# One stage of a fused attention and expert kernel: four of seven products summed in one accumulation bank, groups of products interleaved, result memory opened at another point

## The chip, the cores and the metric

One core of one Trainium2 chip runs the whole kernel as one program. The metric is the time of one execution on the device in microseconds (us). Five engines matter, each with its own queue of instructions that it takes in order: TensorE (PE in the rows; PEld are its weight loads), VectorE (DVE), ScalarE (ACT), GpSimd (POOL) and SyncE (SP, which here only issues transfers). They meet through semaphores.

## The reference, cut to what matters

Attention with normed queries and keys, then a routed expert layer (each token goes to one of 8 experts), then a bilinear layer. The change lies in the bilinear layer alone:

```python
def _moe2_ref(x, w1, w2, w3, w_out):      # x: 1792 x 768
    a = x @ w1                            # 768 x 1024
    b = x @ w2                            # 768 x 1024
    h = a * b @ w3                        # 1024 x 1024
    return (h @ w_out).astype(np.float32) # 1024 x 768
```

## The kernel before, in words

Numbers are carried as pairs of 16-bit floats (high part, low part), so a product of two matrices is three matmuls: high by high, low by high, high by low. `mm3` (line 940) issues these for three blocks of 128 rows, nine matmuls to an accumulation bank ("a product" below). There are eight banks (`mm_p`, tile name psm), handed out in turn; each holds 512 numbers per partition.

`w3 @ w_out` is formed early in the program. The last stage (line 1433, tiles pso) multiplies it by the elementwise product `a * b`, which lies in tiles `ab0` to `ab7`, also as pairs. The stage in front of it, the one that is changed, computes `a` and `b` and their elementwise product. It does so block by block with seven products in the place of eight, after a scheme of sums and differences of the four quarters of each operand. The operand from x is split into quarters by rows of x and by tokens. The seven forms of it are the tiles `b_0` to `b_6` (T1, T2, T3, T4, B11, B21, B22 in the code), and there is a set for each of two groups of tokens: s=0 with 2 x 384 tokens and s=1 with 2 x 512. The set for s=0 is ready before the stage starts, that for s=1 is made in the stage by `operands(1)`: a difference on VectorE (lines 1055, 1065, 1066, 1067, on tile `y`), a high part on ScalarE (line 1050), a low part on VectorE (line 1053). The seven forms of a weight block are the tiles `m2w`, three tiles (j = 0, 1, 2) for each pair (fp, z): fp = 0 to 3 counts blocks of columns, z = 0 stands for w1 and z = 1 for w2. A piece (fp, z, j) is made in four steps: three VectorE instructions rebuild 32-bit numbers from the loaded 64-bit ones (lines 205 to 207, tile `y32w`), four small sums follow (lines 1165 to 1168, on GpSimd, or on VectorE for four early pieces), ScalarE writes the high part (line 1175), and VectorE the low part (line 1182). The pieces of fp = 0 are ready when the stage starts; the other 18 are made in it.

Work that feeds later products is a generator, `steps()`, whose items carry a place ("gate") from which they may be issued and a cost. After each product the code calls `fill(slot, us)`, which lets the generator go on while its gate is reached and a credit of time is left; `force(key)` issues what is missing of a weight block at the point where the first product needs it. What results is the order of each engine's queue, and it is fixed: every instruction stays behind the one written before it on its engine.

Before, `half(fp, s)` does 14 products, one group of seven for z = 0 and one for z = 1, group after group in the order A11, S2, S3, S1, A12, A22, S4. The first four take a bank each. A12, A22 and S4 are then added in the banks of A11, S3 and S1. ScalarE copies the first product out (line 1368, tiles ua and ub), and VectorE forms all sums with it: five additions per group (lines 1329 and 1331) that read a bank. VectorE also multiplies a by b (lines 1349 and 1386), four instructions per half. `done` writes the pair into `ab`: high part on ScalarE (line 1345), low part on GpSimd (line 1346). The tiles `ab1` to `ab7` lie where `y` lay, so `open_ab` can be called only when `operands(1)` has been issued in full.

## Time and profile before

| what | us |
|---|---|
| median of 3 timed runs (967.3 to 971.01) | 970.12 |
| the profiled execution | 965.99 |
| its span in the trace | 964.1 |
| the changed stage in the trace (633.1 to 847.3) | 214.2 |
| the last stage, from there to the end of the span | 116.8 |

Of the span PE is busy 869.6 us (90%), DVE 647.2 (67%), ACT 476.9 (49%) and POOL 310.8 (32%). The rest of the program, before 633 us and after 847 us, is the same text in both kernels. A busy share is an average: in the stage that is changed the question is which engine PE waits for, and when.

### The profile page before, as it was taken

Reading aid. Unit: us, or ns where it says so; the run is one execution under the profiler, and the core shown is the slowest. Engines: PE = TensorE matmul, PEld = TensorE weight load, DVE = VectorE, ACT = ScalarE, POOL = GpSimd, SP = SyncE. Lnnn points to the kernel's source line nnn. Section 1 sums busy time; section 2 is a strip of 40 time slices with the busy share of each in tenths; the row PEclk is TensorE's granted clock in tenths of the full one; section 3 lists DMA queues with packets and bytes.
Section 4 is the critical chain, followed back from the end, with each engine's and each line's share of the span. In section 5 each row is a group of like instructions: output and inputs, shape, how many; then the busy total and the mean of one; then the engine's idle time right before and its main releaser. Section 6 shows DMA issues by size and latency. Waiting matters only on the chain.

```text
span 964.1 us, 19484 instructions
## 1 busy us (share of the span) xinstructions
PE 869.6 (90%) x7766; PEld 588.0 (61%) x7766; DVE 647.2 (67%) x956; ACT 476.9 (49%) x738; POOL 310.8 (32%) x325
## 2 busy tenths in 40 slices
PE   0498899999998979998999999997889899999996
PEld 0155566666665745776889999963444445456664
DVE  6988988878897776255556788999976766220000
ACT  4698788878887543343456766543322222110000
POOL 6367556767743224310101110002333423121111
PEclk9899899999999998999999999998999999999999
DMA  7858689797399974595788999611222211111111
GB/s 184 188 143 203 150 175 199 138 185 160 84 203 217 238 223 135 173 215 170 257 254 244 302 288 289 214 45 38 72 66 66 67 44 50 50 66 50 50 50 50
DMA packets 200351, 144.44 MB, mean 150 GB/s; under 512 B 139376, under 2 KB 178832, under 8 KB 200256
## 3 DMA queue, kind: packets, MB, share of 16 engines
q1 hardware_dynamic: 197248, 131.39, 53.1%
q0 software_dynamic: 3008, 11.76, 3.7%
q8 instruction: 63, 1.03, 0.5%
q14 instruction: 32, 0.26, 0.1%
HBM read 103.52 MB, written 14.18 MB: 122 GB/s over the span
## 4 chain that ended last, share of the span: by engine, by line
PE 41%; DVE 8%; issue 3%; DMA 1%; ACT 0%; POOLq 0%; DVEq 0%; SPq 0%; ACTq 0%
PE psm L940 30%; PE pso L1433 11%; DVE m2w L1182 1%; DVE y32w L206 1%; DVE y32w L205 1%; DVE y32w L207 1%; DMA xte<-xr 1%; DVE ua L1349 0%; DVE ua L1331 0%; DVE u L1331 0%; DVE b L1053 0%; DVE ub L1329 0%; DVE y L1067 0%; DVE y L1055 0%; ACT b L1050 0%
## 5 line engine op out<-in xcount | busy, mean ns | idle before, releaser
L940 PE MATMUL psm<-b,m2w 128*128 128x384 f16 (+1 forms) x1008 | 197.1, 359 | 17.2 <-DVE u L1331 8.9
L940 PEld LDWEIGHTS <-m2w 128*128 128x128 f16 x1008 | 99.9, 99 | 114.1 <-issue 15.7
L940 PE MATMUL psm<-ht,w2t 128*128 128x320 f16 (+7 forms) x1152 | 124.2, 270 | 0.0
L940 PEld LDWEIGHTS <-w1t 128*128 128x128 f16 x1152 | 109.5, 99 | 22.2 <-issue 4.5
L940 PEld LDWEIGHTS <-w2t 128*128 128x128 f16 x1152 | 109.0, 98 | 13.9
L940 PE MATMUL psm<-xte,w1t 128*128 128x288 f16 (+6 forms) x1008 | 106.3, 268 | 6.7 <-PEq L1027 4.2
L1433 PE MATMUL pso<-ww,ab 128*128 128x384 f16 x672 | 109.4, 326 | 0.0
L404 DVE TENSOR_REDUCE nm<-psm 128x2 f32<-128x896 f32 x84 | 88.6, 1084 | 12.9 <-PE psm L402 12.5
L461 PE MATMUL po<-vf,e 128*128 128x65 f32 (+1 forms) x576 | 90.0, 275 | 4.6 <-ACT w L227 4.6
L1433 PEld LDWEIGHTS <-ab 128*128 128x128 f16 x672 | 65.7, 98 | 43.6
L461 PEld LDWEIGHTS po<-vf,e 128*128 128x128 f32 (+1 forms) x576 | 71.2, 180 | 20.4 <-issue 12.1
L402 PE MATMUL psm<-kt,qt 64*64 64x448 f16 x336 | 47.5, 380 | 35.3 <-DMA qt<-qf 28.1
L723 POOL DMA_INDIRECT xr<-xd,ix x19 | 22.3, 1173 | 173.7 <-DMA ix<-md 159.1
L431 PE MATMUL pss<-qt,kt 64*128 64x448 f16 (+1 forms) x576 | 68.3, 379 | 10.6 <-DVE e L446 9.0
L1437 DVE TENSOR_SCALAR ob<-pso,meta_s 128x384 f32<-128x384 f32 x14 | 8.7, 618 | 99.3 <-PE pso L1433 93.4
L1130 DVE SCALAR_TENSOR_TENSOR w1t<-st,w1t 128x1024 f16<-128x1024 f32 x42 | 50.9, 1223 | 35.3 <-ACT w1t L1124 34.0
L464 PE MATMUL po<-v,e 128*128 128x65 f16 (+1 forms) x480 | 63.9, 195 | 1.7 <-DVE lacc L525 1.7
L465 PE MATMUL po<-vl,e 128*128 128x64 f16 (+1 forms) x480 | 63.8, 194 | 0.0
L466 PE MATMUL po<-v,e 128*128 128x65 f16 (+1 forms) x480 | 63.0, 194 | 0.0
L1436 ACT ACTIVATE ob<-pso,meta_s 128x384 f32<-128x384 f32 x14 | 8.1, 580 | 99.0 <-PE pso L1433 99.0
L446 DVE TENSOR_TENSOR e<-pss,e 128x896 f16<-128x896 f32 x48 | 51.7, 1083 | 6.5 <-ACT e L444 6.2
L464 PEld LDWEIGHTS <-e 128*128 128x128 f16 (+1 forms) x480 | 53.1, 115 | 4.7 <-issue 2.9
(266 smaller groups left out, 1647.9 us busy)
## 6 DMA issues: line engine op xcount, KB each, us to landing
st<-in_moe_w_dram SPq DMA_DIRECT2D x42, 512.0 KB, 5.0
st<-in_moe_w_dram SPq DMA_DIRECT2D x44, 384.0 KB, 4.9
st<-in_moe_w_dram SPq DMA_DIRECT2D x48, 256.0 KB, 3.3
w<-in_moe_w_dram SPq DMA_DIRECT2D x16, 512.0 KB, 4.6
w<-in_moe_w_out_dram SPq DMA_DIRECT2D x16, 384.0 KB, 3.8
xd<-rx SPq DMA_DIRECT2D x12, 448.0 KB, 4.1
kf<-in_k_dram SPq DMA_DIRECT2D x24, 192.0 KB, 3.5
qf<-in_q_dram SPq DMA_DIRECT2D x24, 192.0 KB, 3.1
```

Of the source, the lines that this page charges most:

```text
L402: nc.tensor.matmul(ps[h, z, 0:S], lhsT=s["q"][0][h, c:c + 64], rhs=s["k"][0][h, S * j:S * j + S], start=True, stop=True)
L404: nc.vector.tensor_reduce(s["nm"][:, t], ps[:, :, 0:S], axis=AX.X, op=ALU.max, negate=True)
L431: nc.tensor.matmul(ps[o, h, 0:S], lhsT=l, rhs=rt[HD[h], S * j:S * j + S], start=a == 0, stop=a == 3)
L446: nc.vector.tensor_tensor(lo, p, hi, op=ALU.subtract)
L461: nc.tensor.matmul(ov[r, t, :], lhsT=e[0], rhs=vfs[i % 2][:, h, c, 0:D + 1], start=z == 0, stop=z == 3)
L464: nc.tensor.matmul(ov[r, t, :], lhsT=e[0], rhs=vh, start=z == 0, stop=False)
L465: nc.tensor.matmul(ov[r, t, 0:D], lhsT=e[0], rhs=s["vl"][:, h, c, :], start=False, stop=False)
L466: nc.tensor.matmul(ov[r, t, :], lhsT=e[1], rhs=vh, start=False, stop=z == 3)
L723: nc.gpsimd.indirect_dma_start(out=dst, out_offset=None, in_=xd, in_offset=bass.IndirectOffsetOnAxis(ap=ix[0:dst.shape[0], t:t + 1], axis=0))
L940: nc.tensor.matmul(ps, lhsT=x, rhs=y, start=first and j == 0, stop=last and j == n - 1, **kw)
L1130: nc.vector.scalar_tensor_tensor(t[:, 1], st, 32.0, t[:, 0], op0=ALU.mult, op1=ALU.subtract)
L1433: nc.tensor.matmul(pp[z], lhsT=ab[f][:, x, ts], rhs=ww[f][:, y, z * 384:(z + 1) * 384], start=f == 0 and x == 0 and y == 0, stop=f == 7 an ...
```

## The change

A group of seven products now uses three banks. A11, S2, S3 and A22 are added up in one, in this order, and ScalarE copies the running sum out behind each of the first three (and behind A22 for z = 0), line 1340, into tiles named c11, c12, c22 and c21 (all shown as `c` in the rows, with a number). S1 and then S4 are added up in the second, A12 has the third. VectorE makes three additions per group (lines 1344 and 1346): A12 onto c11, S1 onto c22, S1 + S4 onto c12. The multiplications stay four per half (lines 1354 and 1373). The seven products of a group have the places 0, 1, 3, 5, 6, 9 and 11, groups start 7 places apart, and all products are issued in the order of their places, so that two groups alternate on PE: A11, S1, A22 of the group before, S2, S4 of the group before, A12, S3. The gates of z = 1 weight pieces become 25 + 3j in the place of 24 + 4j, and the estimate in `fill` is another one. `open_ab` is called after step 11 of `operands(1)` instead of 12, and results for `ab1` to `ab7` that are ready before that wait in a list (`late`) and are written out one per product afterwards.

The new code, without the removed lines (they stand in the kernel above):

```diff
+            yield 28 * (fp - 1) + (25 + 3 * j if z else 8 + 6 * j if fp > 1 else 0), c
+    ab = [ab0p.tile([P, 2, NT], F16, name="ab0")]
+    pending, late = [], []
+    made_by = {A11: 2, S1: 5, S2: 7, A12: 9, S3: 8, A22: 11, S4: 3}
+    def done(f, cs, x):
+        if f >= len(ab):
+            late.append((f, cs, x))
+            return
+        nc.scalar.activation(ab[f][:, 0, cs], x, AF.Copy)
+        nc.gpsimd.tensor_tensor(ab[f][:, 1, cs], x, ab[f][:, 0, cs], op=ALU.subtract)
+    def group(fp, s, z, a):
+        stt, tt = nc.vector.scalar_tensor_tensor, nc.vector.tensor_tensor
+        c1, c2 = halves(s)
+        n = PC[s][1]
+        r = 1.0 if z else 1.0 / 256
+        bk, x = {}, {}
+        def read(k, name, ps):
+            x[k] = temp(name, s)
+            nc.scalar.activation(x[k], ps, AF.Copy, scale=r)
+        def add(k, ps):
+            if z:
+                tt(x[k], ps, x[k], op=ALU.add)
+            else:
+                stt(x[k], ps, r, x[k], op0=ALU.mult, op1=ALU.add)
+        def end(k, slot):
+            if not z:
+                a[k] = x[k]
+                return
+            def finish():
+                tt(x[k], a[k], x[k], op=ALU.mult)
+                done(fp + 4 * (k >= 2), (c1, c2)[k % 2], x[k])
+            pending.append((slot, finish))
+        def run(slot, p, ps):
+            if p == A11:
+                read(0, "c11", ps)
+            elif p == S2:
+                read(1, "c12", ps)
+            elif p == S3:
+                read(3, "c22", ps)
+                pending.append((slot + 1, lambda: (add(3, bk[1]), end(3, slot + 2))))
+            elif p == A12:
+                add(0, ps)
+                end(0, slot)
+            elif p == S4:
+                add(1, ps)
+                end(1, slot + 1)
+            elif p == A22 and z:
+                tt(a[2], ps, a[2], op=ALU.mult)
+                done(fp + 4, c1, a[2])
+            elif p == A22:
+                read(2, "c21", ps)
+                a[2] = x[2]
+        of = {A11: (0, B11, True), S1: (1, T1, True), S2: (0, T2, False), A12: (2, B21, True), S3: (0, T3, False),
+              A22: (0, T4, False), S4: (1, B22, False)}
+        last = fp == SB - 1 and s and z
+        at = {A11: 0, S1: 1, S2: 3, A12: 6 if last else 5, S3: 5 if last else 6, A22: 9, S4: 11}
+        def product(slot, p):
+            if p == A11:
+                force((fp, z))
+            w = wst2[fp, z]
+            while fp == 0 and s and len(done2) < made_by[p]:
+                one()
+            b, o, first = of[p]
+            if first:
+                bk[b] = bank(n)
+            cs = slice(p * P, (p + 1) * P)
+            mm3(bk[b], [(w[j][:, 0, cs], w[j][:, 1, cs], bt[s][o][:, 0, j], bt[s][o][:, 1, j]) for j in range(3)], first, True,
+                skip_group_check=not first)
+            run(slot, p, bk[b])
+            if len(done2) >= 11 and len(ab) == 1:
+                open_ab()
+            if late and len(ab) > 1:
+                done(*late.pop(0))
+            pending.sort(key=lambda q: q[0])
+            while pending and pending[0][0] <= slot:
+                pending.pop(0)[1]()
+                pending.sort(key=lambda q: q[0])
+            fill(slot, 9 * n * .000425 - (.1 + n * .0006))
+        return [(at[p], p, product) for p in at]
+    line = []
+    for g in range(4 * SB):
+        if g % 2 == 0:
+            a = {}
+        line += [(7 * g + t, p, f) for t, p, f in group(g // 4, g // 2 % 2, g % 2, a)]
+    for slot, p, f in sorted(line, key=lambda q: q[0]):
+        f(slot, p)
+    while pending:
+        pending.pop(0)[1]()
+        pending.sort(key=lambda q: q[0])
```

ScalarE's queue at the start of the stage. Before (ua, a and ub are copies out of a bank; b are high parts of the operands for s=1):

```order
L1368 ACTIVATE ua<-psm 128x384
L1050 ACTIVATE b_4_9769<-y_5815 128x1536
L1050 ACTIVATE b_6_9771<-y_5815 128x1536
L1390 ACTIVATE a_9848<-psm 128x384
L1050 ACTIVATE b_0_9765<-y_5815 128x1536
L1368 ACTIVATE ub<-psm 128x384
L1050 ACTIVATE b_1_9766<-y_5815 128x1536
L1345 ACTIVATE ab_9781<-a_9848 128x384
```

After the change, from the same place:

```order
L1340 ACTIVATE c_9792<-psm 128x384
L1050 ACTIVATE b_4_9769<-y_5815 128x1536
L1050 ACTIVATE b_6_9771<-y_5815 128x1536
L1340 ACTIVATE c_9823<-psm 128x384
L1050 ACTIVATE b_0_9765<-y_5815 128x1536
L1340 ACTIVATE c_9847<-psm 128x384
L1340 ACTIVATE c_9860<-psm 128x384
L1050 ACTIVATE b_1_9766<-y_5815 128x1536
L1340 ACTIVATE c_9884<-psm 128x384
```

The operand copies stay in their order (four of the seven are shown), but beside them stand five copies out of banks in the place of three: they follow A11, S2 and S3 of the first group, A11 of the second and A22 of the first.

VectorE's queue where the last operand form for s=1 (b_3, T4) and the first weight piece of fp=1 (y32w from st_9794) are made. Before:

```order
L1053 TENSOR_TENSOR b_3_9768<-y_5815,b_3_9768 128x1536
L205 TENSOR_SCALAR y32w<-st_9794 128x512
L206 SCALAR_TENSOR_TENSOR y32w<-st_9794,y32w 128x512
L207 SCALAR_TENSOR_TENSOR y32w<-st_9794,y32w 128x512
L1165 TENSOR_TENSOR y32w<-y32w 128x128
L1166 TENSOR_TENSOR y32w<-y32w 128x128
L1167 TENSOR_TENSOR y32w<-y32w 128x128
L1168 TENSOR_TENSOR y32w<-y32w 128x128
L1349 TENSOR_TENSOR c_9823<-c_9823,c_9908 128x384
L1331 SCALAR_TENSOR_TENSOR u_10025<-psm,ua 128x512
```

After the change:

```order
L1053 TENSOR_TENSOR b_3_9768<-y_5815,b_3_9768 128x1536
L1344 TENSOR_TENSOR c_9896<-psm,c_9896 128x384
L205 TENSOR_SCALAR y32w<-st_9794 128x512
L206 SCALAR_TENSOR_TENSOR y32w<-st_9794,y32w 128x512
L207 SCALAR_TENSOR_TENSOR y32w<-st_9794,y32w 128x512
L1165 TENSOR_TENSOR y32w<-y32w 128x128
L1166 TENSOR_TENSOR y32w<-y32w 128x128
L1167 TENSOR_TENSOR y32w<-y32w 128x128
L1168 TENSOR_TENSOR y32w<-y32w 128x128
L1346 SCALAR_TENSOR_TENSOR c_9947<-psm,c_9947 128x512
L1354 TENSOR_TENSOR c_9896<-c_9823,c_9896 128x384
```

Before, the addition u_10025, which frees the bank into which the next product A22 is to be added, stands behind the piece and behind a multiplication. After, the two additions around the piece (c_9896, c_9947) read banks that no later product is added into.

VectorE's queue up to the low part (line 1182) of the last weight piece for fp=1, z=1, the second m2w row in the first fence, the only one in the other. Before:

```order
L1331 SCALAR_TENSOR_TENSOR ua<-psm,ua 128x384
L1331 SCALAR_TENSOR_TENSOR u_10263<-psm,ua 128x384
L1331 SCALAR_TENSOR_TENSOR u_10263<-psm,u_10263 128x384
L1182 SCALAR_TENSOR_TENSOR m2w<-y32w,m2w 128x896
L205 TENSOR_SCALAR y32w<-st_10182 128x512
L206 SCALAR_TENSOR_TENSOR y32w<-st_10182,y32w 128x512
L207 SCALAR_TENSOR_TENSOR y32w<-st_10182,y32w 128x512
L1331 SCALAR_TENSOR_TENSOR c_10262<-psm,ua 128x384
L1331 SCALAR_TENSOR_TENSOR ua<-psm,ua 128x384
L1182 SCALAR_TENSOR_TENSOR m2w<-y32w,m2w 128x896
L1329 TENSOR_TENSOR ub<-psm,ub 128x384
```

After the change:

```order
L1344 TENSOR_TENSOR c_10117<-psm,c_10117 128x512
L205 TENSOR_SCALAR y32w<-st_10175 128x512
L206 SCALAR_TENSOR_TENSOR y32w<-st_10175,y32w 128x512
L207 SCALAR_TENSOR_TENSOR y32w<-st_10175,y32w 128x512
L1346 SCALAR_TENSOR_TENSOR c_10192<-psm,c_10192 128x384
L1354 TENSOR_TENSOR c_10117<-c_9983,c_10117 128x512
L1182 SCALAR_TENSOR_TENSOR m2w<-y32w,m2w 128x896
L1346 SCALAR_TENSOR_TENSOR c_10292<-psm,c_10292 128x384
```

The three instructions of the rebuilding in front of that low part belong to fp=2 in both. Of the additions of the group fp=1, s=0, z=0 five stand in front of it before, and one after.

## Rows read from the trace of the kernel before

**Rows 1.** Stretches: us, busy PE, PEld, DVE, ACT, POOL (count), PE clock, DMA, GB/s

```profile
633.10:847.30 214.20, 196.96 (x1011) 99.90 (x1009) 155.93 (x216) 55.96 (x81) 65.07 (x86) 0.97 0.17 56
...
637.20:707.50 70.30, 59.04 (x299) 29.78 (x296) 65.58 (x88) 22.54 (x28) 17.09 (x20) 0.93 0.21 67
```

**Rows 2.** Timeline of PE in the stage: start, us, what, [idle before <- releaser]

```profile
633.16 8.94 PE L940 MATMUL psm<-b,m2w 128*128 128x384 f16 x54
642.28 21.71 PE L940 MATMUL psm<-b,m2w 128*128 128x384 f16 x117 [0.18 <-DVE u L1331]
669.84 26.71 PE L940 MATMUL psm<-b,m2w 128*128 128x512 f16 x126 [5.85 <-ACT ab L1345]
701.05 5.72 PE L940 MATMUL psm<-b,m2w 128*128 128x384 f16 x25 [4.50 <-DVE u L1331]
707.53 43.78 PE L940 MATMUL psm<-b,m2w 128*128 128x384 f16 x227 [0.76 <-DVE m2w L1182]
753.41 4.22 PE L940 MATMUL psm<-b,m2w 128*128 128x384 f16 x25 [2.09 <-DVE u L1331]
759.40 43.78 PE L940 MATMUL psm<-b,m2w 128*128 128x384 f16 x227 [1.77 <-DVE m2w L1182]
805.27 42.20 PE L940 MATMUL psm<-b,m2w 128*128 128x384 f16 x207 [2.09 <-DVE u L1331]
```

**Rows 3.** Stretches of PE: us, busy (count), PE clock, DMA share, GB/s

```profile
669.00:673.00 4.00, 3.16 (x8) 0.50 0.39 131
757.00:761.00 4.00, 2.23 (x14) 1.00 0.41 135
805.00:809.00 4.00, 3.73 (x16) 0.69 0.00 0
```

**Rows 4.** Timeline of DVE before the first long wait of PE ends

```profile
664.11 1.76 DVE L1053 TENSOR_TENSOR b<-y,b 128x1536 f16<-128x1536 f32 x1 [1.55 <-ACT b L1050]
665.79 0.42 DVE L205 TENSOR_SCALAR y32w<-st 128x512 uint32<-128x512 uint32 x1
...
668.63 0.55 DVE L1349 TENSOR_TENSOR c<-c,c 128x384 f32<-128x384 f32 x1
669.10 0.68 DVE L1331 SCALAR_TENSOR_TENSOR u<-psm,ua 128x512 f32<-128x512 f32 x1
```

**Rows 5.** Timeline of DVE: start of its run, and ends of two waits for fp=1

```profile
637.21 1.75 DVE L1055 TENSOR_TENSOR y<-y 128x1536 f32<-128x1536 f32 x1
...
685.48 1.08 DVE L1182 SCALAR_TENSOR_TENSOR m2w<-y32w,m2w 128x896 f16<-128x896 f32 x1
...
701.10 0.56 DVE L1331 SCALAR_TENSOR_TENSOR u<-psm,u 128x384 f32<-128x384 f32 x1
...
706.14 1.33 DVE L1182 SCALAR_TENSOR_TENSOR m2w<-y32w,m2w 128x896 f16<-128x896 f32 x1
```

**Rows 6.** Groups of DVE by form in 633 to 848: busy us, mean ns, idle before

```profile
L1329 DVE TENSOR_TENSOR ub<-psm,ub 128x512 f32<-128x512 f32 x8 | 5.5, 691 | 6.1 <-PE psm L940 6.0
...
L1331 DVE SCALAR_TENSOR_TENSOR ua<-psm,ua 128x384 f32<-128x384 f32 x8 | 4.4, 555 | 2.3 <-PE psm L940 2.1
```

**Rows 7.** Lines 1182 and 1329 alone: count, shortest/median/longest in ns

```profile
L1182 DVE SCALAR_TENSOR_TENSOR m2w<-y32w,m2w x21: 1080/1089/2053, 619.3 to 807.0; 128x896 f16<-128x896 f32 x21
...
L1329 DVE TENSOR_TENSOR ub<-psm,ub x16: 545/622/692, 646.9 to 847.5; 128x384 f32<-128x384 f32 x8, 128x512 f32<-128x512 f32 x8
```

**Rows 8.** Groups of ACT by form in 633 to 848

```profile
L1175 ACT ACTIVATE m2w<-y32w 128x896 f16<-128x896 f32 x18 | 17.0, 943 | 14.5 <-POOL y32w L1168 11.2 <-DVE y32w L1168 3.3
...
L1390 ACT ACTIVATE a<-psm 128x512 f32<-128x512 f32 x4 | 2.4, 594 | 18.6 <-PE psm L940 18.6
```

**Rows 9.** Timeline of ACT at the start of the stage

```profile
636.08 0.47 ACT L1368 ACTIVATE ua<-psm 128x384 f32<-128x384 f32 x1
636.45 2.85 ACT L1050 ACTIVATE b<-y 128x1536 f16<-128x1536 f32 x2
```

**Rows 10.** Waits in 620 to 850: who for whom, us in total, times, longest

```profile
ACT ab L1345 <- DVE a L1386: 46.8, 8, 7.9
```

More of the change, by code (lines that the diff above doesn't have):

```diff
@@ L1305, in steps @@
             fp, z, j = pieces[min(k, len(pieces) - 1)]
-            yield 28 * (fp - 1) + (24 + 4 * j if z else 8 + 6 * j if fp > 1 else 0), c
-    ab = []
-    ab = []
-    def half(fp, s):
-        stt, tt = nc.vector.scalar_tensor_tensor, nc.vector.tensor_tensor
-        c1, c2 = halves(s)
-        n = PC[s][1]
-        r = 1.0 / 256
-        slot = 14 * (2 * fp + s)
-        us, ev = 9 * n * .000425, .2 + n * .00099
-        def product(ps, w, a, o, first):
-            cs = slice(a * P, (a + 1) * P)
-            while slot == 15 and len(done2) < 7:
-                one()
-            mm3(ps, [(w[j][:, 0, cs], w[j][:, 1, cs], bt[s][o][:, 0, j], bt[s][o][:, 1, j]) for j in range(3)], first, True,
-                skip_group_check=not first)
-        def add(out, ps, x, z):
-            if z:
-                tt(out, ps, x, op=ALU.add)
-            else:
-                stt(out, ps, r, x, op0=ALU.mult, op1=ALU.add)
-        def rest():
-            nonlocal slot
-            while slot == 15 and len(done2) < 12:
-                one()
-            if len(done2) == 12 and len(ab) == 1:
-                open_ab()
-            while pending and pending[0][0] <= slot:
-                finish(*pending.pop(0)[1:])
-            fill(slot, us - ev)
-            slot += 1
-        def done(f, cs, x):
-            nc.scalar.activation(ab[f][:, 0, cs], x, AF.Copy)
-            nc.gpsimd.tensor_tensor(ab[f][:, 1, cs], x, ab[f][:, 0, cs], op=ALU.subtract)
-        def finish(f, cs, x, y):
-            tt(x, x, y, op=ALU.mult)
-            done(f, cs, x)
-        a = {}
-        def end(z, k, x):
-            if z:
-                when = slot + 1 if fp or s else {(0, 1): 14, (1, 0): 15, (1, 1): 17}[k]
-                pending.append((when, fp + 4 * k[0], (c1, c2)[k[1]], a[k], x))
-                pending.sort(key=lambda p: p[0])
-            else:
-                a[k] = x
-        for z in range(2):
-            force((fp, z))
-            w = wst2[fp, z]
-            p1 = bank(n)
-            product(p1, w, A11, B11, True)
-            u = temp("ub" if z else "ua", s)
-            nc.scalar.activation(u, p1, AF.Copy, scale=1.0 if z else r)
-            rest()
-            ps = bank(n)
-            product(ps, w, S2, T2, True)
-            add(u, ps, u, z)
-            rest()
-            p3 = bank(n)
-            product(p3, w, S3, T3, True)
-            x21, t1 = temp("c21", s), temp("u3", s)
-            add(t1, p3, u, z)
-            rest()
-            p4 = bank(n)
-            product(p4, w, S1, T1, True)
-            add(t1, p4, t1, z)
-            end(z, (1, 1), t1)
-            rest()
-            product(p1, w, A12, B21, False)
-            if z:
-                tt(a[0, 0], p1, a[0, 0], op=ALU.mult)
-                done(fp, c1, a[0, 0])
-            else:
-                a[0, 0] = temp("a11", s)
-                nc.scalar.activation(a[0, 0], p1, AF.Copy, scale=r)
-            rest()
-            product(p3, w, A22, T4, False)
-            add(x21, p3, u, z)
-            end(z, (1, 0), x21)
-            rest()
-            product(p4, w, S4, B22, False)
-            add(u, p4, u, z)
-            end(z, (0, 1), u)
-            rest()
@@ L1401, in fused_kernel @@
-    pending = []
-    ab.append(ab0p.tile([P, 2, NT], F16, name="ab0"))
+            yield 28 * (fp - 1) + (25 + 3 * j if z else 8 + 6 * j if fp > 1 else 0), c
+    ab = [ab0p.tile([P, 2, NT], F16, name="ab0")]
+    pending, late = [], []
+    made_by = {A11: 2, S1: 5, S2: 7, A12: 9, S3: 8, A22: 11, S4: 3}
     def open_ab():
@@ L1410, in open_ab @@
             ab.append(abp.tile([P, 2, NT], F16, name=f"ab{f}"))
-    work = steps()
-    for fp in range(SB):
-        for s in range(2):
-            half(fp, s)
-    for p in pending:
-        nc.vector.tensor_tensor(p[3], p[3], p[4], op=ALU.mult)
-        nc.scalar.activation(ab[p[1]][:, 0, p[2]], p[3], AF.Copy)
-        nc.gpsimd.tensor_tensor(ab[p[1]][:, 1, p[2]], p[3], ab[p[1]][:, 0, p[2]], op=ALU.subtract)
+    def done(f, cs, x):
[4 more added lines that the diff above has]
+        nc.gpsimd.tensor_tensor(ab[f][:, 1, cs], x, ab[f][:, 0, cs], op=ALU.subtract)
```

## The prediction

> **What bounds the kernel now.** I looked first at the stretch that the change touches, then at who waits there. The reader is to see that PE is the engine that sets the end: in the 214.2 us of the stage it is busy for 197.0, VectorE for 155.9, ScalarE for 56.0 and GpSimd for 65.1 [rows 1]. The timeline of PE shows the waits in brackets [rows 2]: 0.18 + 5.85 + 4.50 + 0.76 + 2.09 + 1.77 + 2.09 = 17.24 us.
>
> What the stage costs without a wait comes from one row: 227 matmuls in 43.78 us [rows 2] (that at 759.40). They are 101 with 384 columns and 126 with 512 (the count from the start of the stage gives the mix), 103,296 columns, so 0.4238 ns per column. A block fp is 126 x 384 + 126 x 512 = 112,896 columns, 47.85 us; four blocks are 191.4 us. The stage runs from 633.16 to 847.47, the end of the last row of [rows 2]: 214.3 us. So 22.9 us are lost, and no rearrangement of this stage can give more, as the matmuls stay the same in number and size. 17.24 are waits. The other 5.7 are matmuls at the low clock behind waits: by the column price the row at 669.84 (45 with 384 columns, 81 with 512) should take 24.90 and takes 26.71, the row at 701.05 (25 with 384) 4.07 against 5.72, the row at 805.27 (81 and 126) 40.52 against 42.20. That is 1.7 to 1.8 us each. The granted clock is 0.50 at 669 (1.2 of 2.4 GHz) behind the wait of 5.85, averages 0.69 at 805 behind one of 2.09, but stays at 1.00 around the wait of 1.77 [rows 3].
>
> Who is late is VectorE. The wait of 5.85 carries ScalarE's name, but it ends at 669.84, just behind an addition of VectorE that ran from 669.10 to 669.78; in front of this stood the last operand form (664.11), a whole weight piece (from 665.79) and a multiplication [rows 4]. Likewise the wait of 4.50 ends 0.05 us before the addition at 701.10 begins, its predecessor having just freed the bank, and the wait of 0.76 at 707.53 just behind a low part that ended at 706.14 + 1.33 = 707.47 [rows 2, 5]. From 637.2 to 707.5 VectorE is busy for 65.58 of 70.30 us [rows 1]: until there the stage runs at VectorE's pace, afterwards at PE's, with three waits of 2 us.
>
> **The change part by part.**
>
> *Additions leave VectorE.* Per half there are 10 instead of 14 additions and multiplications: 4 x 8 = 32 fewer. What counts is the run up to that low part of fp=1, z=1, which I call the turn. Up to it the queue before holds 14 + 14 + 5 = 33 of them, the new one 10 + 10 + 1 = 21, and the same seven rebuilt pieces and the same operand work. The 12 that go are 8 with 384 columns at 0.555 us and 4 with 512 at 0.691 [rows 6]: 4.4 + 2.8 = 7.2 us. VectorE's idle time up to there is 70.30 - 65.58 = 4.7 us. Of this I let about 0.8 go, because fewer of its instructions wait for a product just issued; some stays, since the operand forms still go to and fro between VectorE and ScalarE. The turn then comes at 707.5 - 7.2 - 0.8 = 699.5. Bounds: 695.6, if all idle time goes too; 707.5, if new waits on VectorE eat the whole saving.
>
> GpSimd's subtractions are not fewer (32 before and after). The low parts of line 1182 take 1.09 us in the median and up to 2.05, while an addition that reads a bank never takes over 0.69 [rows 7]. So what goes is the sort that is never stretched, and I take it at its clean price. The Trainium skill ("SBUF — State Buffer", section "Who interferes with whom") has a rule for this: a VectorE instruction with at most one input in SBUF does not contend with GpSimd, and one with two such inputs is blocked for the whole of a GpSimd instruction that reads there. The rows agree. Were all instructions stretched alike instead, the 12 would save up to 7.2 x 2.05 / 1.09 = 13.5 us, and the turn would come up to 6 us earlier.
>
> *Reads go to ScalarE.* 32 more copies out of banks at up to 0.594 us [rows 8] are at most 19 us on an engine that is busy for 56 of 214. Their sum is hidden; what can cost is their place, as S2, S3 and A22 now each wait for a copy. Between them PE has two other products (2 x 9 x 384 x 0.4238 ns = 2.9 us, or 3.9 with 512 columns). In front of the copy may stand a high part of 0.94 us [rows 8] or an operand copy of 1.43 (2.85 for two, [rows 9]). At the start that doesn't fit: PE begins at 633.16, has A11 and S1 done at 636.1, but ScalarE takes its first copy at 636.08 to 636.55 behind a high part, so S2 waits for 0.5 us. S3 then waits for a copy behind the two operand copies, which end at 639.4 with the copy at 639.9, against 639.5 on PE: 0.4 to 0.5. I take 1.0 us for the start; the bounds are 0 and the 2.85 of both operand copies. Both ends vanish in the stretch up to the turn, which VectorE sets.
>
> *What PE has left at the turn.* Before, it resumes at 707.53 with 252 + 70 matmuls behind it. In the new order A22 and S4 of that group come later, so it has 18 fewer: 252 + 52, that is 112,896 + 52 x 384 = 132,864 columns of 451,584. Left are 318,720 columns, 135.1 us.
>
> *Behind the turn.* The waits at 753.41, 759.40 and 805.27 go. Two of them were for additions that free a bank [rows 2]; now the only addition before a product into the same bank is S1's, with four products in between. The third was for a low part of fp=2; in the new order that still stands behind a piece of fp=3, so I leave 0.5 us for it (bounds: 0 and the 1.77 of before). PE reaches the turn's weights before they are there: VectorE ended fp=1, z=0 at 685.48 + 1.08 = 686.6 [rows 5]; 7 of its additions and multiplications in front of that go (4 x 0.555 + 3 x 0.691 = 4.3 us) and a little idle time, so about 682. PE is there at 679 (633.16 + 1.0 + 14 products of 1.465 + 12 of 1.953 us + 7 matmuls), so it waits for 2 to 3 us. Then it needs 0.3 + 4 x 1.465 + 2 x 1.953 + 1.1 = 11.2 us more to the turn, arrives at 693.2, and waits for some 6. Behind such a wait one more fall of the clock is to be paid, 1.7 us.
>
> *The rest.* Opening the result memory one step earlier and holding two results back keeps two of the eight temporaries longer; both are free before the queue comes round to them. The changed gates are contained in the orders shown. The order within the last group and the last stage's start cost nothing: its first six column blocks use results of s=0 alone, some 45 us of matmuls.
>
> **The sum.** 699.5 + 135.1 + 1.7 + 0.5 = 836.8, against 847.3 before: 10.5 us less. From the profiled execution's 965.99 that makes 955.5. That execution is 4.1 us under the median of the timed runs, 970.12, which the result will be compared with: 959.6.
>
> **The rivals.**
> *VectorE is no longer late* (PE-bound throughout). For it speaks that VectorE's total falls to some 136 us against 191 of PE; against it that 58 us of work stand in the 62 up to the turn. The stage would be 191.4 + 1.0: 21.9 less, 948.
> *The turn stays where it was*: VectorE's saving turns into waits for PE and ScalarE, or is eaten by GpSimd's subtractions, which come at other moments. For it: the stretching up to 2.05 us [rows 7]. Then 707.5 + 137.3 = 844.8, 2.5 less, 967.6.
> *Slower: ScalarE becomes the link that PE waits for.* ScalarE takes its queue in order, and before it stood for 46.8 us in front of result copies that wait for a multiplication on VectorE [rows 10]. Now such copies stand in front of bank reads. There are 16 groups x 3 = 48 links; from 22.9 / 48 = 0.48 us of waiting at each the whole possible gain is gone. At 0.66 us it is 31.7 us on 191.4, 223.1 for the stage, 8.8 more: 979. Against it: by the durations above the copies come in time nearly everywhere but at the start. The Trainium skill ("TensorE: Matmul & The Clock Gate", section "A second HAM failure mode: psum-queue depth-cycling") speaks for it too: a kernel that cycles through banks can idle between groups of matmuls so often that the clock falls again and again. With a fall of 1.7 us in each of the 16 groups another 27 us would come on top, 1006. The trace bears out only falls behind waits of 2 us and more.
>
> **How the numbers follow.** The forecast has 0.72, with its own range of 954 to 964; VectorE not late 0.12; the turn unmoved 0.11; slower 0.05. The range 948 to 966 takes in the first two and ends short of the third. About 0.5% (4.9 us) is what a measurement of this kernel can tell from no change: the first two cases are faster by more, the third is within, the fourth slower. So 0.84, 0.11, 0.05.
>
> **What would show it.** In the new trace PE should wait for 0.5 to 1 us in the first 7 us of the stage with ScalarE as releaser, about 2 us before the first product of fp=1, some 6 us before that of fp=1, z=1 with line 1182 as releaser, ending near 699.5, and hardly afterwards; the wait before A22 at 664 to 670 is gone. The prediction is wrong if line 1340 releases many waits, if the low part of the turn ends after 704 or before 695, or if waits of over 1 us stand behind it.

## The result, and the profile after

The changed kernel takes 961.9 us (median of 11 runs, 958.06 to 965.97), the kernel before on the same chip 970.12 us (11 runs, 966.25 to 974.44): a ratio of 0.9916, with a 95% interval of 0.9889 to 0.9943. That is 8.2 us less; 10.5 were forecast, and 959.6 us. The interval leaves out 1, so the change is faster, by less than 1%. Some executions on a chip are a slower sort, and the ratios here and in the table below leave them out: two of the six of e10, none of the other runs.

The timeline of PE through the stage in the changed kernel answers to [rows 2] (start, busy time, line, tiles, count of matmuls; in brackets the wait in front and what ended it):

```profile
640.10 3.09 PE L940 MATMUL psm<-b,m2w 128*128 128x384 f16 x18
643.54 42.63 PE L940 MATMUL psm<-b,m2w 128*128 128x384 f16 x223 [0.36 <-ACT c L1340]
688.56 8.77 PE L940 MATMUL psm<-b,m2w 128*128 128x384 f16 x47 [2.38 <-DVE m2w L1182]
699.65 4.05 PE L940 MATMUL psm<-b,m2w 128*128 128x384 f16 x16 [2.32 <-ACT c L1340]
704.78 47.84 PE L940 MATMUL psm<-b,m2w 128*128 128x384 f16 x252 [1.08 <-DVE m2w L1182]
754.73 88.91 PE L940 MATMUL psm<-b,m2w 128*128 128x384 f16 x452 [2.11 <-DVE m2w L1182]
843.48 56.71 PE L1433 MATMUL pso<-ww,ab 128*128 128x384 f16 x348
```

The stage runs from 640.10 to 843.48, 203.4 us; before it was 214.3. The waits are 8.25 us instead of 17.24, and no addition in a bank is waited for any more. What is lost beside the waits is 203.4 - 191.4 - 8.25 = 3.7 us, before 5.7.

The windows of the stage and of its part up to the turn, in the changed kernel (length; then busy us and count of PE, its weight loads, VectorE, ScalarE and GpSimd; granted clock), answer to [rows 1]:

```profile
640.10:843.48 203.38, 194.97 (x1011) 99.27 (x1009) 132.61 (x185) 72.06 (x114) 67.66 (x85) 0.98 0.18 59
640.10:704.73 64.63, 58.39 (x306) 29.89 (x303) 62.02 (x84) 28.56 (x40) 17.22 (x18) 0.97 0.21 70
```

From the stage's start to the turn, the window of the kernel before (633.16 to 707.47) has 74.31 us with VectorE busy for 69.49 in 95 instructions. So VectorE lost 7.5 us of work and 4.82 - 2.61 = 2.2 us of idle time, and the turn (the end of the low part for fp=1, z=1 that PE waits for) comes 9.7 us earlier. The remaining 1.2 us of the 11 are saved behind it.

Two rows of ScalarE and four of VectorE show what the wait of 2.32 us in front of the turn was. A22's multiplication (line 1373) stood in VectorE's queue behind a rebuilt piece; the result copy of line 1324 waits for it, and the copy out of the bank that PE needs stands behind that copy:

```profile
698.59 0.63 ACT L1324 ACTIVATE ab<-c 128x512 f16<-128x512 f32 x1 [3.07 <-DVE c L1373]
699.13 0.47 ACT L1340 ACTIVATE c<-psm 128x384 f32<-128x384 f32 x1
```

```profile
697.87 0.68 DVE L1373 TENSOR_TENSOR c<-psm,c 128x512 f32<-128x512 f32 x1
...
703.39 1.34 DVE L1182 SCALAR_TENSOR_TENSOR m2w<-y32w,m2w 128x896 f16<-128x896 f32 x1
...
750.22 1.53 DVE L207 SCALAR_TENSOR_TENSOR y32w<-st,y32w 128x512 uint32<-128x512 uint32 x1
...
753.34 1.34 DVE L1182 SCALAR_TENSOR_TENSOR m2w<-y32w,m2w 128x896 f16<-128x896 f32 x1
```

The low part at 703.39 is the turn's, ending at 704.73. That at 753.34 is the one PE waits for at fp=2, z=1; in front of it stand the rebuilding of fp=3's first piece (748.76 to 751.75) and three additions and multiplications.

One thing hides part of the gain in this execution: the stage begins 6.94 us later than in the execution before, though the instructions up to there are the same. In the first expert PE pauses, and the profile names nothing that it waits for ("issue"):

```profile
392.19 0.57 PE L940 MATMUL psm<-xt,w1t 128*128 128x320 f16 x3 [0.63 <-issue]
394.32 0.43 PE L940 MATMUL psm<-xt,w1t 128*128 128x320 f16 x2 [1.56 <-issue]
...
396.44 9.17 PE L940 MATMUL psm<-xt,w1t 128*128 128x320 f16 x54 [1.10 <-issue]
```

Such pauses are in 5 of the 14 profiles of this study. Therefore the experiments are read by the stage: its length, and the turn counted from its start.

### The profile page after: what moved, and what is told of

It is laid out like the page before. It is cut to its first block, busy times and chain, and to the rows that moved or that the text cites. A ratio compares the mean times of both kernels' runs of the same rounds, so it can differ in the third digit from the quotient of the medians.

```text
span 960.3 us, 19438 instructions
## 1 busy us (share of the span) xinstructions
PE 872.9 (91%) x7766; PEld 590.6 (62%) x7766; DVE 624.3 (65%) x924; ACT 492.5 (51%) x770; POOL 315.5 (33%) x325
## 4 chain that ended last, share of the span: by engine, by line
PE 42%; DVE 7%; issue 2%; ACT 1%; POOLq 0%; ACTq 0%
PE psm L940 31%; PE pso L1433 11%; DVE m2w L1182 1%; DVE y32w L207 1%; DVE y32w L206 1%; DVE y32w L205 1%; DVE c L1354 1%; DVE c L1344 0%; DVE b L1053 0%; DVE c L1346 0%; ACT b L1050 0%; DVE y L1067 0%; DVE w1t L1130 0%; DVE y32w L1165 0%; ACT c L1340 0%
## 5 line engine op out<-in xcount | busy, mean ns | idle before, releaser
L940 PE MATMUL psm<-b,m2w 128*128 128x512 f16 (+1 forms) x1008 | 195.1, 356 | 8.4 <-DVE m2w L1182 5.6
L461 PE MATMUL po<-vf,e 128*128 128x65 f32 (+1 forms) x576 | 93.1, 282 | 4.6 <-ACT w L227 4.6
L1325 POOL TENSOR_TENSOR ab<-c,ab 128x384 f16<-128x384 f32 (+1 forms) x32 | 39.1, 1232 | 155.4 <-ACT ab L1324 152.1
L461 PEld LDWEIGHTS po<-vf,e 128*128 128x128 f32 (+1 forms) x576 | 73.7, 186 | 21.0 <-issue 12.6
L464 PE MATMUL po<-v,e 128*128 128x65 f16 (+1 forms) x480 | 65.1, 198 | 1.7 <-DVE lacc L525 1.7
L466 PE MATMUL po<-v,e 128*128 128x65 f16 (+1 forms) x480 | 64.1, 195 | 0.0
L1324 ACT ACTIVATE ab<-c 128x384 f16<-128x384 f32 (+1 forms) x32 | 18.2, 575 | 81.7 <-DVE c L1354 72.7
```

Of the source, the lines that this page charges most:

```text
L461: nc.tensor.matmul(ov[r, t, :], lhsT=e[0], rhs=vfs[i % 2][:, h, c, 0:D + 1], start=z == 0, stop=z == 3)
L464: nc.tensor.matmul(ov[r, t, :], lhsT=e[0], rhs=vh, start=z == 0, stop=False)
L466: nc.tensor.matmul(ov[r, t, :], lhsT=e[1], rhs=vh, start=False, stop=z == 3)
L940: nc.tensor.matmul(ps, lhsT=x, rhs=y, start=first and j == 0, stop=last and j == n - 1, **kw)
L1325: nc.gpsimd.tensor_tensor(ab[f][:, 1, cs], x, ab[f][:, 0, cs], op=ALU.subtract)
```

## The experiments

The stage's length runs to the first matmul of the last stage; "idle" is VectorE's idle time up to the turn; waits are PE's in the stage. The ratio is to the kernel before on the same chip, with its interval. All columns but the ratio are read from one profiled execution per run. A fall of the clock more or less is worth 1.4 to 2.9 us in these profiles, so differences of that size in the stage alone say little.

| run | stage, us | turn | VectorE busy + idle up to it | waits | ratio |
|---|---|---|---|---|---|
| before | 214.3 | 74.3 | 69.5 + 4.8 | 17.2 | |
| changed | 203.4 | 64.6 | 62.0 + 2.6 | 8.3 | 0.9916 (0.9889 to 0.9943) |
| e0 changed, again | 203.3 | 64.6 | 62.0 + 2.6 | 9.5 | 0.9885 (0.9850 to 0.9919) |
| e1 no overlap | 234.5 | 72.8 | 62.0 + 10.8 | 34.5 | 1.0196 (1.0150 to 1.0242) |
| e2 VectorE reads | 210.9 | 70.7 | 69.2 + 1.5 | 15.3 | 0.9980 (0.9950 to 1.0011) |
| e3 more additions | 214.0 | 70.0 | 67.2 + 2.7 | 16.7 | 1.0025 (0.9998 to 1.0052) |
| e4 copies later | 206.3 | 64.9 | 62.5 + 2.4 | 9.8 | 0.9903 (0.9872 to 0.9933) |
| e5 low part first | 202.5 | 61.3 | 58.5 + 2.8 | 9.8 | 0.9876 (0.9845 to 0.9908) |
| e6 sums on GpSimd | 202.7 | 62.3 | 58.2 + 4.0 | 7.2 | 0.9871 (0.9834 to 0.9907) |
| e7 both | 203.3 | 61.5 | 53.2 + 8.3 | 9.0 | 0.9897 (0.9860 to 0.9934) |
| e8 old pace | 214.2 | 73.3 | 61.1 + 12.2 | 14.5 | 0.9993 (0.9962 to 1.0025) |
| e10 gates | 199.3 | 64.6 | 62.0 + 2.6 | 5.7 | 0.9861 (0.9794 to 0.9928) |
| e11 gates, sums | 196.9 | 62.3 | 58.3 + 4.0 | 5.1 | 0.9829 (0.9780 to 0.9877) |
| e12 and copies later | 198.8 | 62.5 | 59.6 + 3.0 | 5.6 | 0.9882 (0.9843 to 0.9921) |

**e0, the changed kernel again.**

> The changed kernel once more, as it is, on the chip of the next three. Its first profile shows 6 us in the first expert, at 388 to 396 us, in which PE stands still for no reason that the profile names, and a stage that begins at 640.1, while four kernels with the same code up to there began it at 627.8 to 632.8. Theory (that was this one execution): no such pause, stage from 628 to 634, stage length again 203.4 within 0.7, turn 64.6 us after its start within 0.4, waits for line 1182 of 2.4, 1.1 and 2.1 us. Rival (the pause belongs to this kernel): stage from 638 or later. If the clock falls in other places, the stage may differ by 1.5 us without the waits differing.

No pause, stage from 633.17 (before: 633.16), 203.3 us long. The timed runs gave 953.94 against 964.88 us, 10.9 less. The forecast of 10.5 us was one of the stage; a pause in one of the two kernels' executions takes from it or adds to it.

One expected wait was missed: the wait for the low part at the turn is 2.37 us instead of 1.1.

```profile
692.71 2.76 PE L940 MATMUL psm<-b,m2w 128*128 128x384 f16 x16 [2.32 <-ACT c L1340]
697.83 49.52 PE L940 MATMUL psm<-b,m2w 128*128 128x384 f16 x252 [2.37 <-DVE m2w L1182]
749.45 87.23 PE L940 MATMUL psm<-b,m2w 128*128 128x384 f16 x452 [2.09 <-DVE m2w L1182]
```

The 16 matmuls in front of the turn took 2.76 us here and 4.05 at the low clock in the first profile. PE arrived 1.3 us earlier, and the turn stayed where it was, 64.6 us after the stage's start: PE's pace in front of it does not set it.

**e1, groups one behind the other.**

```diff
-        at = {A11: 0, S1: 1, S2: 3, A12: 6 if last else 5, S3: 5 if last else 6, A22: 9, S4: 11}
+        at = {A11: 0, S1: 1, S2: 2, A12: 3, S3: 4, A22: 5, S4: 6}
```

> The seven products of a group stand one directly behind the other again; four of them still share a bank and ScalarE still copies behind each. In the changed kernel the stage takes 203.4 us (640.10 to 843.48) and the low part that ends the turn is over 64.6 us after the stage's start. Theory (the overlap is what hides ScalarE's copies): A22 now goes into a bank directly behind S3, whose copy takes 0.47 to 0.6 us, so PE waits some 0.75 us with line 1340 as releaser in each of 16 groups. Up to the turn five of them, 3.8 us, are taken out of the waits for line 1182 that stand there anyway (2.4 + 1.1 us), so the turn moves by under 1.5 us; behind it 11 x 0.75 = 8 us are added: stage 211 to 213, total 8 to 10 us over the changed kernel, about that of the kernel before. Rival 1 (the copies are short, and the overlap is not needed): stage 202.5 to 204.5. Rival 2 (ScalarE's queue, with result copies and high parts in front of the copies, makes every link cost over 1.2 us): stage over 219, slower than the kernel before.

31 us more, over three times what I expected. PE's waits in the stage, by what ended them (total, times, longest):

```profile
PE psm L940 <- ACT c L1340: 19.0, 17, 3.9
PE psm L940 <- DVE c L1344: 11.1, 8, 1.7
PE psm L940 <- DVE c L1346: 3.4, 3, 1.5
PE psm L940 <- DVE m2w L1182: 1.0, 2, 0.5
```

The link to ScalarE costs what I had put, 0.74 to 0.78 us in most groups. I had overlooked a second one: S4 goes into the bank that the addition behind S3 still reads, 14.5 us in 11 waits. Two of ScalarE's took 3.87 and 3.35 us; there the copy stands behind a high part that had waited 4.89 and 4.37 us for GpSimd's sums. Rival 2 named the right size, but its reason holds for such waits only. The overlap is what keeps both links off the path.

**e2, VectorE reads the banks.**

```diff
-            nc.scalar.activation(x[k], ps, AF.Copy, scale=r)
+            nc.vector.tensor_scalar(x[k], ps, r, None, op0=ALU.mult)
```

> Banks are shared and groups overlapped as in the changed kernel, but VectorE instead of ScalarE copies the banks' contents (56 copies more on VectorE, 56 fewer on ScalarE). Theory (what the change gave is VectorE's time up to the turn): up to the low part of fp=1, z=1 there are 17 copies more on VectorE at 0.55 to 0.69 us, 9.5 to 11.5 us, against 6.2 us of waits of PE there; the turn goes from 64.6 us after the stage's start to 73 to 76 and the stage from 203.4 to 212 to 215 us, all of the gain and perhaps more given back. Rival (the gain comes from the shared banks and from the order of the products, whichever engine copies): stage 203 to 206, turn where it was.

The turn goes back by 6.1 us, less than expected: the 17 copies up to it take 10.2 us by their rows, but VectorE's busy time grows by only 7.2, and 1.1 us of idle time go. The stage is 7.5 us longer. The rival's 203 to 206 is excluded. Some of the gain stays: VectorE has as much work up to the turn as in the kernel before (69.2 against 69.5 us), and the turn still comes 3.6 us earlier, with 1.5 us of idle time instead of 4.8. That part belongs to the shared banks, the order of the products and the new pace together.

**e3, 32 more additions.**

```diff
                 stt(x[k], ps, r, x[k], op0=ALU.mult, op1=ALU.add)
+            if k < 2:
+                stt(x[k], ps, 0.0, x[k], op0=ALU.mult, op1=ALU.add)
```

> 32 additions more on VectorE, each directly behind one of the 32 of z=0 (bank and sum in, sum out; they add the bank times zero, so the values stay). Nothing else is changed. Theory (until the turn the stage goes at VectorE's pace, one for one): nine of them come before the low part of fp=1, z=1, five with 384 columns at 0.555 and four with 512 at 0.69 us, 5.5 us; the turn goes from 64.6 to 69.5 to 70.5 us after the stage's start, the stage from 203.4 to 207.5 to 210. Rival (VectorE is no longer what sets the turn; ScalarE's copies or PE do): turn and stage within 1.5 us of the changed kernel.

The window up to the turn:

```profile
627.80:697.75 69.95, 60.21 (x306) 30.36 (x304) 67.24 (x93) 28.65 (x40) 17.30 (x20) 0.95 0.22 68
```

5.2 us more work in nine more instructions, the turn 5.3 us later: one for one, as the theory said. The stage grew by 10.6 us, though, and 214.0 lies outside the expected range. The other half stands behind the turn, where PE waits for line 1340 for 0.81, 0.81 and 1.53 us and for line 1182 for 3.61. There VectorE is not the pace as a whole, but its lateness reaches PE through ScalarE's queue: result copies wait for a multiplication (86.2 us in this kernel, 72.7 in the changed one), and copies out of banks stand behind them. So in front of the wait that ends at 736.99: the result copy at 735.83 had waited 6.71 us for the multiplication, and the two copies out of banks follow it at 736.36.

**e4, result copies later.**

```diff
-                done(fp + 4 * (k >= 2), (c1, c2)[k % 2], x[k])
+                pending.append((slot + 2, lambda: done(fp + 4 * (k >= 2), (c1, c2)[k % 2], x[k])))
```

(The same for the copy behind A22.)

> The copies of results on ScalarE (and the subtraction on GpSimd behind each) are issued two places later, so that copies out of banks stand in front of them in ScalarE's queue. In the changed kernel PE waits 2.32 us at 697.3 us for such a copy (line 1340), which stands behind a result copy, which waits for VectorE; then 1.08 us for the low part that ends the turn. Theory (VectorE sets the turn, PE's wait for ScalarE in front of it costs nothing of its own): the wait of 2.32 us goes and the wait for line 1182 at the turn grows to 2.5 to 3.4 us; the turn stays at 64.6 us after the stage's start within 0.7, the stage at 203.4 within 1.2. Rival (ScalarE's queue in order is part of what sets the time): the turn comes 1.5 to 2.3 us earlier, or waits behind it shrink, stage 200 to 201.8.

The wait of 2.32 us is gone, and the turn stays:

```profile
681.72 11.73 PE L940 MATMUL psm<-b,m2w 128*128 128x384 f16 x63 [3.08 <-DVE m2w L1182]
697.77 50.78 PE L940 MATMUL psm<-b,m2w 128*128 128x384 f16 x252 [4.32 <-DVE m2w L1182]
750.57 88.74 PE L940 MATMUL psm<-b,m2w 128*128 128x384 f16 x452 [2.01 <-DVE m2w L1182]
```

So ScalarE's wait had cost nothing of its own. The stage is 2.9 us longer than in the changed kernel all the same: the clock. Behind one wait of 4.32 us, 252 matmuls take 50.78 us; in the changed kernel 47.84. Granted was 0.50 (1.2 of 2.4 GHz) for the first 4 us and 0.75 in the next:

```profile
697.80:701.80 4.00, 4.00 (x13) 1.92 (x14) 2.23 (x4) 1.85 (x3) 2.97 (x5) 0.50 0.24 79
701.80:705.80 4.00, 4.00 (x20) 2.13 (x19) 0.00 (x0) 0.60 (x2) 1.01 (x3) 0.75 0.37 122
```

**e5, e6 and e7, less in front of the turn.** e5 makes a block's last low part before the next block's first piece is rebuilt; e6 puts all small sums on GpSimd; e7 does both.

```diff
+            if t and n > 6 and k % 3 == 0:
+                yield k - 1, 0
+                stage_lower(t.pop(0))
+                yield k, 1.1
...
-            own_ = fp == 1 and j != 1
+            own_ = False
```

> VectorE makes the low part of a block's last weight piece before it rebuilds the next block's first piece; in the changed kernel it is the other way round, and the rebuilding (2.2 us at 700.07 to 702.23, 3.0 us at 748.76 to 751.75) stands ahead of the low part that PE waits for. Theory (the mis-sized late wait of 2.11 us is that order, and nothing else): the turn comes 2 to 2.5 us earlier after the stage's start (62.2 to 62.6), the wait before fp=2, z=1 and its clock fall (1.6 us) go, stage 203.4 - 2.2 - 2.1 - 1.6 = 197.5, at most 199.5 if some clock fall stays. Rival (the low part brought forward only waits for ScalarE's high part, 0.95 us behind a queue, and holds VectorE up): turn within 0.7 of 64.6 or later, stage 202.5 to 206.

> The four small sums of each of the pieces of fp=1 that VectorE made itself (four pieces, 16 sums of 0.28 to 0.29 us, 0.95 us a piece) go to GpSimd, where such a set takes about 2.5 us. Theory (VectorE's time up to the turn counts, one for one): the turn comes 3.0 to 3.8 us earlier, 60.8 to 61.6 us after the stage's start; behind it the wait of 2.1 us before fp=2, z=1 stays; stage 199.5 to 200.5. Rival (the high part on ScalarE then waits for GpSimd and holds back ScalarE's copies out of the banks, and the low part comes no earlier): turn within 1 us of 64.6 or later, stage 202.5 or more, with waits for line 1340 of 1 us and more.

> Both together: the low part of a block's last piece before the next block's first piece, and all small sums on GpSimd. Theory (both act through VectorE's time up to the turn, and add): turn 5 to 6 us earlier, 58.6 to 59.6 us after the stage's start; PE can't be there before 11.2 + 48.2 = 59.4 without waits, so nearly all waits are gone and the stage goes at PE's pace: 193 to 196, against a floor of 191.4; total 7 to 10 us under the changed kernel. Rival (GpSimd's sums, now 2.5 us behind each rebuilt piece, are the next thing late): stage 198 or more, waits for line 1182 of over 2 us stay.

Each brought the turn 2.3 to 3.3 us forward, and no more when both were done; the stage gained 0.0 to 0.8 us, which one profile each does not tell from nothing. Here my theories failed, in the stage all three and in the turn e6's and e7's. In e6 both waits for low parts stay, 2.33 us at the turn and 2.08 behind it; VectorE has 3.8 us less work up to the turn but 1.4 more idle time, and a fall of the clock stands behind the turn. In e5 PE waits for no low part any more, but for copies out of banks, in front of the turn and in every block behind it (line 1344 there is 1340 here):

```profile
683.40 6.97 PE L940 MATMUL psm<-b,m2w 128*128 128x512 f16 x36 [1.71 <-ACT c L1344]
693.22 10.40 PE L940 MATMUL psm<-b,m2w 128*128 128x384 f16 x63 [2.85 <-ACT c L1344]
704.52 30.78 PE L940 MATMUL psm<-b,m2w 128*128 128x384 f16 x153 [0.91 <-ACT c L1344]
735.95 11.40 PE L940 MATMUL psm<-b,m2w 128*128 128x512 f16 x63 [0.65 <-ACT c L1344]
748.09 6.01 PE L940 MATMUL psm<-b,m2w 128*128 128x384 f16 x36 [0.74 <-ACT c L1344]
755.34 30.78 PE L940 MATMUL psm<-b,m2w 128*128 128x384 f16 x153 [1.24 <-ACT c L1344]
```

The waits of 1.71 and 2.85 us in front of the turn come through result copies that had waited 5.93 and 3.08 us for VectorE. Behind the turn GpSimd has a part: ScalarE in e5 ahead of two of the waits, at 735.95 and 755.34. The high part of line 1175 waits for GpSimd's sums, and the copies stand behind it:

```profile
733.95 0.95 ACT L1175 ACTIVATE m2w<-y32w 128x896 f16<-128x896 f32 x1 [6.71 <-POOL y32w L1168]
734.81 0.61 ACT L1328 ACTIVATE ab<-c 128x512 f16<-128x512 f32 x1
735.33 0.96 ACT L1344 ACTIVATE c<-psm 128x512 f32<-128x512 f32 x2
...
753.58 0.95 ACT L1175 ACTIVATE m2w<-y32w 128x896 f16<-128x896 f32 x1 [5.16 <-POOL y32w L1168]
754.44 0.85 ACT L1344 ACTIVATE c<-psm 128x384 f32<-128x384 f32 x2
```

In e7 ScalarE waits 38.6 us for GpSimd's sums, and VectorE's 8.8 us less of work turn into 5.7 us more of idle time.

**e8, the old numbers of the pace.**

```diff
-            yield 28 * (fp - 1) + (25 + 3 * j if z else 8 + 6 * j if fp > 1 else 0), c
+            yield 28 * (fp - 1) + (24 + 4 * j if z else 8 + 6 * j if fp > 1 else 0), c
...
-            fill(slot, 9 * n * .000425 - (.1 + n * .0006))
+            fill(slot, 9 * n * .000425 - (.2 + n * .00099))
```

> The changed kernel with the old numbers of the pace: gates 24 + 4j for the pieces of z=1, and .2 + n x .00099 us per addition in the credit, so that the pieces are spread over more products. Theory (VectorE's sum of work up to the turn decides, and the last low part is issued by force in front of the product that needs it, with either numbers): turn within 1 us of 64.6 us after the stage's start, stage 202.4 to 205. Rival (the new numbers of the pace are a part of the gain): with the same additions gone, turn at 67 or later and stage 206 or more.

The rival holds: the whole gain of the stage is gone. Up to the turn VectorE has the same 84 instructions and even a little less busy time, and the turn is 8.7 us later:

```profile
641.33:714.63 73.30, 60.81 (x306) 30.28 (x303) 61.12 (x84) 28.87 (x40) 17.43 (x17) 0.89 0.18 58
```

Pieces are left until the product that needs them forces them out, two at a time. Then VectorE rebuilds while PE waits, and as PE works off its products VectorE has nothing to do. The run puts back both numbers at once, gates and credit, so it does not tell one from the other; and the kernel before with the new numbers was not run, so what they would give without the rest stays open. On PE:

```profile
690.04 1.14 PE L940 MATMUL psm<-b,m2w 128*128 128x384 f16 x3 [2.84 <-DVE m2w L1182]
694.01 13.27 PE L940 MATMUL psm<-b,m2w 128*128 128x384 f16 x59 [2.83 <-DVE m2w L1182]
708.33 0.34 PE L940 MATMUL psm<-b,m2w 128*128 128x384 f16 x1 [1.05 <-ACT m2w L1175]
711.78 1.14 PE L940 MATMUL psm<-b,m2w 128*128 128x384 f16 x3 [3.11 <-DVE m2w L1182]
714.69 50.29 PE L940 MATMUL psm<-b,m2w 128*128 128x384 f16 x252 [1.78 <-DVE m2w L1182]
```

and on VectorE, in the middle of that:

```profile
694.59 0.69 DVE L1354 TENSOR_TENSOR c<-c,c 128x512 f32<-128x512 f32 x1
700.50 0.69 DVE L1373 TENSOR_TENSOR c<-psm,c 128x512 f32<-128x512 f32 x1 [5.21 <-PE psm L940]
```

**e10, gates alone, and e11, with the sums.** After e5 I looked for another way to remove the late wait: the pieces of z=1 are issued four places earlier for fp=2 and fp=3, and the last low part of fp=2, z=1 at place 60.

```diff
-            yield 28 * (fp - 1) + (25 + 3 * j if z else 8 + 6 * j if fp > 1 else 0), c
+            yield 60 if k == 12 and c > 1.5 else 28 * (fp - 1) + ((25 if fp == 1 else 21) + 3 * j if z else 8 + 6 * j if fp > 1 else 0), c
```

> Gates alone: the pieces of fp=2, z=1 four places earlier and the low part of their last piece at place 60 instead of by force at 63. VectorE then has the rebuilding of fp=3's first piece (3.0 us) behind it, and two additions fewer in front of the low part that PE waits for. The orders of VectorE and ScalarE up to the turn are those of the changed kernel. Theory (the late wait of 2.1 us before fp=2, z=1 is that order alone, and ScalarE's copies have room there): turn 64.6 us after the stage's start within 0.4; the late wait under 0.5 us and the clock's fall behind it (1.6 us) gone: stage 203.35 - 3.7 = 199.7, at most 200.5. Rival (as where the low part was put ahead of the rebuilding: the wait is only handed to ScalarE's copies, behind a high part that waits for GpSimd's sums): waits for line 1340 behind the turn of 0.6 us and more, 3 us in all, stage 202 to 204.

> The same gates, and all small sums on GpSimd (alone, these brought the turn from 64.6 to 62.3 us after the stage's start, the stage from 203.35 to 202.65, with 2.75 us of waits for line 1340 in front of the turn). Theory (the two act in different stretches and add): turn 62.3 within 0.5, no wait over 0.5 us behind it: stage 202.65 - 3.7 = 199.0, 198.3 to 199.8. Rival (GpSimd has no room for sums at the earlier places): new waits behind the turn, stage 201 or more.

e10's theory holds. So does e11's for the turn and the waits behind it; its stage came out shorter than its range. In e10 PE runs from the turn to the end without a wait, 704 matmuls in 134.75 us (135.1 were forecast for a clean run), and the stage is 199.3 us:

```profile
701.70 134.75 PE L940 MATMUL psm<-b,m2w 128*128 128x384 f16 x704 [0.69 <-DVE m2w L1182]
836.28 64.03 PE L1433 MATMUL pso<-ww,ab 128*128 128x384 f16 x393
```

e11 adds the sums on GpSimd and came out at 196.9, 1.4 us below its range. The range took over e6's stage, in which the clock fell behind the wait at the turn (252 matmuls took 49.52 us; 47.84 in the changed kernel); in e11 it did not fall there, which I had not foreseen:

```profile
699.69 134.73 PE L940 MATMUL psm<-b,m2w 128*128 128x384 f16 x704 [2.35 <-DVE m2w L1182]
834.26 65.98 PE L1433 MATMUL pso<-ww,ab 128*128 128x384 f16 x405
```

It is the best version here by the ratio and by the stage: 953.06 us, where the kernel before took 969.32. Its interval and that of the changed kernel (e0) overlap a little, so the timed runs don't separate the two. The stage, one profile each, is 6.4 us shorter: 2.3 by the turn, 2.1 by the late wait, and 2.0 by matmuls behind the turn that ran without a fall of the clock.

**e12, e11 with result copies later.**

> The last kernel (gates, and all small sums on GpSimd) with result copies issued two places later on ScalarE. In it PE waits in front of the turn for 1.73 and 0.68 us for copies that stand behind a high part and a result copy on ScalarE, and then 2.35 us for the low part; VectorE has 4.0 us of idle time up to the turn, 1.2 of it behind such a copy. Theory (VectorE sets the turn, and ScalarE counts only as far as it makes VectorE idle): the waits of 0.68 us and more for line 1340 shrink by some 1 us, the wait at the turn grows to 2.3 to 4, the turn comes 0 to 1.2 us earlier (61.1 to 62.3 after the stage's start); if the clock falls behind the longer wait, 1.5 to 3 us are lost again: stage 196 to 199 against 196.9. Rival (ScalarE's order is by now what sets the time): stage 194 to 195.5.

The turn stays (62.5, just outside the range), the wait in front of it grows to 3.16 us, and the 704 matmuls take 136.39 us, a clock fall more. The two waits for copies shrink only from 2.41 to 2.09 us in all. As in e4, ScalarE's order is not the limit there, and the stage is 1.9 us longer.

## Why the prediction was right, point by point

- **The stage**: 203.6 us forecast, 203.4 measured. Two errors cancel in it, 1.7 us at the turn and 1.4 behind it, so that it comes so close is luck; that the gain is made at the turn, by VectorE, is not.
- **The turn**: 66.3 us after the stage's start forecast (699.5 - 633.16), 64.6 measured. (The bounds of 695 and 704 are to be read from the stage's start too: the low part ends at 704.73 in the profile, 697.8 by the clock of the kernel before.) VectorE's work fell by 7.5 us, and 7.2 were put at the clean price; that the removed additions had been stretched like the rest (13.5) is out. Its idle time fell by 2.2 us instead of 0.8. That work of VectorE up to there moves the turn one for one is shown by e3; e2 undoes ScalarE's part and gives 6.1 of the 9.7 us back. That additions leave is not enough: e8 has them gone as well and idles for 12.2 us, e1 for 10.8. I had read the changed gates out of the order and let them stand at no cost; rightly for the sum, but the gain hangs on the new pace and on the overlap as much as on the additions. e8, 73.3 us after the stage's start, lands near where the bound of 707.5 stood (74.3), "new waits on VectorE eat the whole saving".
- **Behind the turn**: 137.3 us forecast, 138.7 measured. The mis-sized term is the late wait before fp=2, z=1: 0.5 us put, 2.11 measured; the bound of 1.77 was too low. The 1.7 us for a fall of the clock were right in sum and not in place: in the first profile the clock fell behind the late wait and not behind that at the turn, in e0 as forecast. e10 shows that the late wait comes from the place of those pieces alone: with other gates it is gone, and the stage is 4.1 us shorter, 2.0 of them by the clock. My sign of a wrong prediction, a wait of over 1 us behind the turn, was there; it fell on a term, not on the mechanism.
- **PE's waits up to the turn**: start 0.36 (0.5 to 1.0 forecast), before fp=1 2.38 (2 to 3), before fp=1, z=1 1.08 (2.37 in e0) instead of 6. The difference is no gain of its own: 2.32 us were spent before S3, on the copy behind S2 on ScalarE, which I had not seen, 1.45 on a clock fall behind it (none in e0), and 1.7 are the earlier turn. e4 takes the wait of 2.32 away, and the one for line 1182 becomes 4.32.
- **The rivals**: that VectorE is no longer late did not come about: 5.6 us of the waits are for line 1182. That ScalarE becomes the link PE waits for did not either, 2.7 us of waits for line 1340 in all, and the clock fell behind two waits, not in each group. But e5 and e7 show how near it is: as soon as the high part comes up earlier than GpSimd's sums, ScalarE's queue hands the wait to PE. That the turn stays nearly unmoved is what e8 does.
- **The total** is 2.3 us above the forecast. The pause in the first expert, where the two kernels' code is the same, can account for that, and in e0 the difference was 10.9 us; that the pause was in the timed runs is not shown, and why it comes in some executions stays open.

## What to carry to other kernels

Take the work up to the moment at which a late engine is caught up, busy and idle time apart: removed instructions shorten the first, and only the order in which the rest is issued decides whether the second grows. When a wait is taken out, look at what stands behind the waiting instruction on an in-order engine, since that is where it reappears; issuing the same steps a few products earlier (e10) cured what an exchange of two steps (e5) only handed on. Where executions differ by several us ahead of the change, compare the stage, not the total.
